# Weights cast to bf16 inside GpSimd DMAs, a shared head for two FFN blocks, and scan PSUM in two slots

## The chip, the cores and the metric

One core of one Trainium2 chip. The metric is the device time of one execution in microseconds (us), lower is better. Executions of one kernel mostly agree within 0.3%, though in this case several kernels spread more, so comparisons use the fast runs and carry a 95% interval. A run more than 1.5% above the fastest of its kernel is called slow and is left out of ratios.

## The reference, cut to what matters

A Mamba-2 scan (4 batches, 8 heads, 768 tokens, head size 32, state size 16), whose output, 3,072 tokens of 256 channels, goes through a feed-forward network (FFN) with a squared ReLU.

```python
for c in range(nc):                      # chunks of 32 tokens
    M = einsum(Cc, Bc) * L               # L: causal mask times decays
    y = M @ xc + (Cc @ state) * exp(cum)
    state = decay_full * state + sum(B x * decay_from_j)
x = y.transpose(0, 2, 1, 3).reshape(3072, 256)
h = np.maximum(x @ w_in, 0.0)            # w_in  256 x 2048, float32, 2.1 MB
out = (h * h) @ w_out                    # w_out 2048 x 256, float32, 2.1 MB
```

## The kernel before

It works in 12 blocks of 256 tokens. For each block GpSimd prepares `cz`, `Bb`, `xs` in bf16; TensorE transposes (`tr`), VectorE copies the result out of PSUM (`bct`); TensorE makes `U` (state input) and `mt` (the C·B products); VectorE makes the state `S` and the masks `mts`; TensorE adds up `Y`; ScalarE copies it out as `T`, the FFN's input. The FFN of a block is eight steps. A step is a group of four products with w_in (`mm1`), a ReLU on ScalarE, a square on VectorE, and, LAG steps later, a group of four with w_out (`mm2`). The scan of block k is strewn among the FFN steps of block k-1, starting LEAD steps ahead.

```python
LAG, LEAD = 4, 12
ps_h = pool(bufs=2)   # PSUM, FFN up-projection      (cut to what matters)
ps_o = pool(bufs=2)   # PSUM, FFN down-projection
ps_s = pool(bufs=1)   # PSUM, scan: ONE slot of four banks
...
def load_wi(f0, f1):  # float32 into a staging tile, SyncE's queue
    nc.sync.dma_start(out=w_in_f[:, :, f0*128:f1*128], in_=...)
def cast_wi(f0, f1):
    nc.scalar.copy(out=w_in_b[...], in_=w_in_f[...])
def cast_wo(f0, f1):
    nc.gpsimd.tensor_copy(out=w_out_b[...], in_=w_out_f[...])
...
# all on SyncE's queue, which moves them in this order
load_wi(0, 2); load_wi(2, 4); ph_load(1); load_wi(4, 8); load_wo(0, 4)
load_wi(8, 12); ph_load(2); load_wi(12, 16)
load_wo(4, 8); load_wo(8, 12); load_wo(12, 16); ph_load(3)
...
for s in range(len(steps) + LAG):
    if s < len(steps):
        mm1(*steps[s])
    for fn, args in todo.pop(s, []):     # scan pieces, casts
        fn(*args)
    if 1 <= s <= len(steps):
        square(*steps[s - 1])
    if LAG <= s < len(steps):
        mm2(*steps[s - LAG])
```

## Time and profile before

| | before |
|---|---|
| median (3 runs, when predicted) | 131.44 us (131.12 to 132.25) |
| span of the profiled execution | 129.1 us |
| TensorE busy | 116.4 us, 90% of the span |
| first FFN product | 14.06 us |
| a steady block of 256 tokens | 8.90 us, TensorE busy in all of it |

Below, the head is the first 34 us or so, in which weights arrive and the scan starts up, and the steady part is what follows. One row that the prediction did not look at, of this kernel's table of 40 slices (each digit is the clock granted to TensorE in tenths of full speed), is needed later:

```profile
PEclk9999999999999999999999999999999999999999
```

### The profile page before, as it was taken

To read this page: it belongs to the slowest core of one execution; us is meant where nothing else is said; L and a number is where in the kernel's file an instruction comes from. 1 tells how busy PE (TensorE), PEld (TensorE's weight loads), DVE (VectorE), ACT (ScalarE), POOL (GpSimd) and SP (SyncE) were. 2 spreads that over 40 slices of the span, in tenths; PEclk is the share of its full clock that TensorE was granted. 3 is DMA by queue.
4 is the path that set the end of the run, shared out by engine and by line. 5 is a ranking of instruction groups with operands and counts; after the bars stand their busy time and mean duration, and the time that the engine had idled before them with its cause. 6 is when DMAs were issued, how large, how long until landed. Compare 5 with 4: busy or idle time off the path is not lost.

```text
span 129.1 us, 4225 instructions
## 1 busy us (share of the span) xinstructions
PE 116.4 (90%) x1776; PEld 90.8 (70%) x1776; DVE 90.9 (70%) x203; ACT 75.6 (59%) x132; POOL 33.2 (26%) x56
## 2 busy tenths in 40 slices
PE   6697675896799999999999999999999999999980
PEld 4444443574687788778787877887787788788850
DVE  1338698499595796895995986977967848654421
ACT  2422784646357658467476576574775765776830
POOL 4045333659540051060150070440600000000000
PEclk9999999999999999999999999999999999999999
DMA  4999989988900550831903805607401020020201
GB/s 91 239 220 286 300 176 303 322 151 180 188 7 5 136 110 5 179 70 40 202 9 95 152 2 121 128 5 160 87 30 59 5 84 0 5 81 0 86 25 57
DMA packets 43172, 14.20 MB, mean 110 GB/s; under 512 B 37840, under 2 KB 40976, under 8 KB 43152
## 3 DMA queue, kind: packets, MB, share of 16 engines
q1 hardware_dynamic: 41712, 13.47, 44.9%
q10 hardware_dynamic: 1440, 0.45, 1.7%
q8 instruction: 14, 0.23, 0.8%
q14 instruction: 6, 0.05, 0.1%
HBM read 10.77 MB, written 3.15 MB: 108 GB/s over the span
## 4 chain that ended last, share of the span: by engine, by line
PE 69%; DVE 9%; SPq 9%; DMA 7%; ACT 2%; issue 1%; DVEq 0%; ACTq 0%
PE ops L334 29%; PE hps L314 27%; SPq L119 8%; DMA w_in_f<-in_moe_w_in_dram 4%; DVE mts L210 4%; DVE h L324 3%; PE Y L286 3%; PE mt L199 3%; DMA B_nat<-in_B_dram 3%; PE Y L274 3%; PE tr L187 2%; PE U L234 1%; PE ops L347 1%; PE tr L185 1%; ACT hb L318 1%
## 5 line engine op out<-in xcount | busy, mean ns | idle before, releaser
L318 ACT ACTIVATE hb<-hps 128x512 bf16<-128x512 f32 x96 | 57.5, 599 | 34.6 <-PE hps L314 33.1
L314 PE MATMUL hps<-T,w_in_b 128*128 128x256 bf16 x384 | 57.7, 273 | 2.0 <-ACT w_in_b L135 1.3
L334 PE MATMUL ops<-w_out_b,h 128*128 128x256 bf16 x368 | 55.5, 273 | 0.1
L324 DVE TENSOR_TENSOR h<-hb 128x512 bf16<-128x512 bf16 x96 | 46.1, 501 | 6.7 <-ACT hb L318 6.6
L314 PEld LDWEIGHTS <-w_in_b 128*128 128x128 bf16 x384 | 37.1, 98 | 7.2 <-ACT w_in_b L135 2.0
L334 PEld LDWEIGHTS <-h 128*128 128x128 bf16 x368 | 33.2, 98 | 7.0 <-issue 2.2
L210 DVE TENSOR_TENSOR mts<-mt,cb 128x512 bf16<-128x512 f32 x46 | 30.5, 685 | 4.5 <-PE mt L199 2.5
L146 POOL TENSOR_TENSOR cz<-C_nat,P_sb 128x256 bf16<-128x256 f32 x11 | 7.5, 679 | 42.0 <-DMA C_nat<-in_C_dram 36.1
L189 DVE COPY bct<-tr 128x768 bf16<-128x768 bf16 x12 | 6.7, 558 | 13.7 <-PE tr L187 13.7
L166 POOL TENSOR_TENSOR xs<-x_nat,Pinv 128x512 bf16<-128x512 f32 x12 | 13.5, 1125 | 9.4 <-DVE Pinv L409 5.1
L390 PE MATMUL dps<-dum 128*128 128x256 bf16 x36 | 7.6, 379 | 1.1 <-DVE dum L382 1.1
L303 ACT CAST T<-Y 128x512 bf16<-128x512 f32 x11 | 6.4, 586 | 2.1 <-PE Y L286 1.0
L160 POOL CAST Bb<-B_nat 128x128 bf16<-128x128 f32 x22 | 6.9, 343 | 2.2 <-DMA B_nat<-in_B_dram 1.2
L274 PE MATMUL Y<-bct,S 32*32 32x128 bf16 x160 | 4.4, 217 | 2.6 <-DVE mts L210 2.5
L390 PEld LDWEIGHTS <-dum 128*128 128x128 bf16 x36 | 4.5, 136 | 2.8 <-DVE dum L382 1.0
L359 ACT COPY osb<-ops 128x512 f32<-128x512 f32 x11 | 6.4, 580 | 0.0
L274 PEld LDWEIGHTS <-S 32*32 32x32 bf16 x160 | 2.5, 90 | 5.2 <-issue 4.8
L286 PE MATMUL Y<-mts,xs 64*32 64x128 bf16 x384 | 5.2, 219 | 0.8 <-DVE mts L216 0.8
L185 PE MATMUL tr<-cb,Bb 128*128 128x128 bf16 x24 | 4.9, 227 | 1.1 <-ACT T L303 1.1
L138 POOL CAST w_out_b<-w_out_f 128x1024 bf16<-128x1024 f32 x4 | 4.2, 1040 | 6.5 <-DMA w_out_f<-in_moe_w_out_dram 6.5
L187 PE MATMUL tr<-cb,cz 128*128 128x128 bf16 x48 | 5.6, 226 | 0.0
L199 PE MATMUL mt<-bct 32*64 32x256 bf16 x192 | 5.5, 291 | 0.0
(39 smaller groups left out, 46.5 us busy)
## 6 DMA issues: line engine op xcount, KB each, us to landing
x_nat<-in_x_dram SPq DMA_DIRECT2D x12, 256.0 KB, 4.4
out_dram<-osb SPq DMA_DIRECT2D x11, 256.0 KB, 2.2
w_out_f<-in_moe_w_out_dram SPq DMA_DIRECT2D x4, 512.0 KB, 6.5
C_nat<-in_C_dram SPq DMA_DIRECT2D x12, 128.0 KB, 4.0
w_in_f<-in_moe_w_in_dram SPq DMA_DIRECT2D x3, 512.0 KB, 5.6
B_nat<-in_B_dram SPq DMA_DIRECT2D x11, 128.0 KB, 3.9
w_in_f<-in_moe_w_in_dram SPq DMA_DIRECT2D x2, 256.0 KB, 4.9
B_nat<-in_B_dram ACTq DMA_DIRECT2D x1, 128.0 KB, 3.3
```

The lines of the kernel that those rows point to most:

```text
L119: (eng or nc.sync).dma_start(out=dst, in_=_dap(src, (b * NH * S + j * 256) * w, [[2 * w, 128], [S * w, NH], [1, 2 * w]]))
L166: eng.tensor_tensor(out=_fap(xs, 0, [[256, 2], [32, 8], [1, 32]]), in0=_fap(loaded[k]["x"], 0, [[32, 2], [64, 8], [1, 32]]), in1=_fap(Pinv ...
L187: nc.tensor.transpose(tr[:, r, 1 + g, :], v["cz"][:, r, 112 * g:112 * g + 128], eye_b)
L199: nc.tensor.matmul(mt[64 * u:64 * u + 64, q, r, :, :], bct[32 * q:32 * q + 32, r, 0, u * 64:u * 64 + 64], _fap(bct[32 * q:32 * q + 32], 12 ...
L210: nc.vector.tensor_tensor(out=v["mts"][:, q], in0=v["mt"][:, q], in1=_fap(cb, 128, [[128, 2], [0, 2], [1, 128]]), op=ALU.mult)
L274: nc.tensor.matmul(Y[u][32 * q:32 * q + 32, g, :], S_b[32 * q:32 * q + 32, g * 32:(g + 1) * 32], _fap(v["bct"][32 * q:32 * q + 32], 128 + ...
L286: nc.tensor.matmul(Y[u][32 * q:32 * q + 32, g, :], v["xs"][64 * u:64 * u + 64, r, h * 32:h * 32 + 32], v["mts"][64 * u:64 * u + 64, q, r, ...
L314: nc.tensor.matmul(hps[:, i, :], w_in_b[:, g, f * 128:(f + 1) * 128], T[blk][:, g].rearrange("p r u t -> p (r u t)"), start=(g == 0), stop ...
L318: nc.scalar.activation(out=hb, in_=hps, func=AF.Relu)
L324: nc.vector.tensor_tensor(out=h2, in0=hb, in1=hb, op=ALU.mult)
L334: nc.tensor.matmul(ops[blk][:, r, :], h2[:, i, r * 128:(r + 1) * 128], w_out_b[:, f, :], start=(f == 0 and r == 0), stop=(f == 15), skip_g ...
L390: nc.tensor.matmul(dps, dum[:, 0:128], dum, start=True, stop=True, skip_group_check=True)
```

## The change

Its intent: ScalarE and GpSimd no longer cast the weights, since the DMA does it; two FFN blocks share the first weights, so that they are needed half as fast; and the scan's PSUM is two slots of two banks, so that one phase of the scan need not wait until the other's tile is empty. With it come a reordered prologue, squares one step later, and a scan that starts two steps later. Below, "lag 1" and "lag 2" say how many steps after its ReLU a square is issued (the constant LAG, for the down-projection, stays 4), and "lead 12" and "lead 10" give LEAD.

```diff
-    LEAD = 12
+    LEAD = 10
-    ps_s = pool(bufs=1)                      # four banks
+    ps_s = pool(bufs=2)                      # two banks each; mt is two tiles
     def load_wi(f0, f1):
-        nc.sync.dma_start(out=w_in_f[...], ...)
+        nc.gpsimd.dma_start(out=w_in_b[...], ...)      # load_wo likewise
-    def cast_wi(...), cast_wo(...), and all their calls
...
         ph_load(1); ph_load(2); ph_load(3)   # SyncE: weights no longer in between
         for i in range(3):
             nc.gpsimd.memset(cz[i], 0.0)
+        load_wi(0, 4); load_wi(4, 8); load_wo(0, 4)
...
         prep_c(1, nc.gpsimd); prep_b(1, nc.gpsimd); prep_x(1, nc.gpsimd)
+        load_wi(8, 16); load_wo(4, 8); load_wo(8, 16)
...
-        warm(14) ... warm(3) ... warm(4) ... warm(3) ... warm(12)
+        warm(15) ... warm(4) ... warm(5, 128) ... warm(14, 128)
...
+        head = [(0, 0), (0, 1), (0, 2), (0, 3), (0, 4), (1, 0), (1, 1), (1, 2), (1, 3),
+                (0, 5), (1, 4), (0, 6), (1, 5), (0, 7), (1, 6), (1, 7)]
+        steps = head + [(b, f) for b in range(2, NPAIR) for f in range(8)]
...
-            if 1 <= s <= len(steps):
-                square(*steps[s - 1])
+            if 2 <= s < len(steps) + 2:
+                square(*steps[s - 2])
```

Cut: the second state of block 0 and one reciprocal moved to later, the first mask taken from its own PSUM tile, positions of block 2's scan pieces.

## The prediction

> **What bounds the kernel now.** I read the page's per-slice table first, then windows, the chain of waits, and a timeline of the first 34 us. The slices (columns are fortieths of the span, 3.23 us each, in tenths busy):
>
> ```profile
> PE   6697675896799999999999999999999999999980
> DVE  1338698499595796895995986977967848654421
> DMA  4999989988900550831903805607401020020201
> ```
>
> The reader is to see two kernels. From slice 12 on TensorE is full and nothing else matters; before it TensorE has holes and the DMA engines are the row that is full. The windows put microseconds on it (start:end, length, then busy time and count for PE, PEld, DVE, ACT, POOL, then clock, DMA share, GB/s):
>
> ```profile
> 0.00:14.00 14.00, 10.43 (x118) 6.45 (x118) 6.17 (x18) 4.42 (x10) 4.87 (x12) 1.00 1.01 223
> 14.00:24.00 10.00, 6.68 (x119) 4.49 (x120) 7.05 (x14) 7.32 (x12) 4.11 (x6) 1.00 0.98 261
> 24.00:33.00 9.00, 7.10 (x125) 5.39 (x122) 8.17 (x14) 4.78 (x9) 6.93 (x11) 1.00 0.92 191
> ...
> 50.50:59.40 8.90, 8.90 (x152) 7.11 (x151) 7.38 (x17) 5.74 (x11) 2.19 (x4) 1.00 0.42 90
> ...
> 122.80:129.10 6.30, 2.52 (x21) 1.63 (x18) 1.08 (x3) 0.97 (x2) 0.00 (x0) 1.00 0.12 42
> ```
>
> A steady block of 256 tokens takes 8.90 us with TensorE busy for all of it. So what the change does after about 34 us is worth nearly nothing; the game is in the first 34 us, where TensorE is idle 3.3 + 1.9 us in the two middle windows, plus whatever the 14 us of prologue can be shortened by (its 10.43 us busy are mostly dummy warm-up products). The timeline names the holes:
>
> ```profile
> 8.96 1.07 ACT L417 CAST mts<-mt 128x512 bf16<-128x512 f32 x2 [2.66 <-PE mt L199]
> 10.07 1.29 DVE L210 TENSOR_TENSOR mts<-mt,cb 128x512 bf16<-128x512 f32 x2 [2.05 <-ACT mts L417]
> ...
> 12.97 0.41 PE L286 MATMUL Y<-mts,xs 64*32 64x128 bf16 x30 [0.80 <-DVE mts L216]
> ...
> 14.06 0.60 PE L314 MATMUL hps<-T,w_in_b 128*128 128x256 bf16 x4 [0.69 <-DVE T L299]
> ...
> 19.49 1.22 DVE L324 TENSOR_TENSOR h<-hb 128x512 bf16<-128x512 bf16 x1
> ...
> 21.36 0.29 PE L274 MATMUL Y<-bct,S 32*32 32x128 bf16 x8 [1.36 <-DVE mts L210]
> ```
>
> ```profile
> 31.72 0.29 PE L274 MATMUL Y<-bct,S 32*32 32x128 bf16 x8 [1.13 <-DVE mts L210]
> ...
> 33.10 0.22 PE L185 MATMUL tr<-cb,Bb 128*128 128x128 bf16 x1 [0.74 <-ACT T L303]
> ```
>
> To be seen: in the prologue VectorE's first mask waits 2.05 us, until ScalarE has copied the other half of the same PSUM tile; the FFN's first product starts at 14.06; block 1's Y products wait for VectorE's masks until 21.36 and block 2's until 31.72; the next transposes wait for the one PSUM tile to be emptied. In the list of waits the casts of w_in on ScalarE also hold TensorE: 2.0 us in 3 waits on the weight-load side, 1.3 us in 3 on the product side, overlapping. None of them is in the steady part.
>
> **What the Trainium skill says.** (1) "TensorE: Matmul & The Clock Gate", Part 1: a warm product costs N / 2.4 GHz plus about 2.5 ns, so 256 columns 109 ns and a group of four 0.437 us. The trace agrees: the chain alternates FFN groups every 0.44 us. (2) "DMA: Bandwidth & Descriptors", section SWDGE vs HWDGE vs iDMA: a cast in the DMA must come from GpSimd, whose cores write the descriptors; the Specifications give a first byte after about 1 us against 0.6. The kernel before has no such DMA, so no trace shows it yet. (3) The same page, "Issuing engines are not separate DMA queues": all queues share the same 16 DMA engines. The DMA row agrees: two queues are in use at the start, and the sum is full. (4) "SBUF — State Buffer", Who interferes with whom: a VectorE instruction with two SBUF inputs contends with a GpSimd one that reads SBUF. The trace agrees: the square at 19.49 took 1.22 us instead of about 0.42 while GpSimd's xs (19.37 to 20.43) ran.
>
> **The change part by part.**
>
> *Casts removed.* ScalarE loses two casts of 0.62 us and three of 1.04 us, 4.4 us; GpSimd four of 1.04 us, 4.2 us. ScalarE's lie in the head and hold TensorE in part. HBM still has to give 4 MB of f32, so the reading side of the DMA does not shrink: over 0 to 27 us it moved about 6.5 MB at 240 GB/s (from the windows). The order changes: scan inputs first on the SP queue, 1.5 MB of weights beside them from GpSimd at about 2.1 us (end of its memsets), the other 2.5 MB only after block 1's preparation on GpSimd.
>
> *Prologue.* The f32 constants go first on ScalarE's queue instead of second: the transposes of the decay waited for them until 5.2, now about 0.5 to 0.7 us less. Masks: the products' output is now two tiles, so the first mask need not wait for ScalarE's copies. Chain after the products, worked from the rows: mask 0.65, state 0.28, mask 0.65, two bf16 masks 0.74, about 2.5 us with handovers, so Y can start near 11.5 where everything before stays in place, against 12.97: 1.4 us. With the constants 2.0; I take 1.8 because new waits will show. First FFN product: 14.06 becomes about 12.3.
>
> *From the first FFN product to block 1's Y.* Before: 7.3 us (14.06 to 21.36), set by VectorE: T copy, bct 0.56, three small state operations 0.8, four masks 2.75, three squares and the contention. The new lag of two steps takes one square (0.42) out of this chain and some of the contention (0.8); the postponed second state of block 0 puts 0.55 back. About 6.4 us, so 0.9 gained. But TensorE now has only the five first groups of block 0 queued before that Y, where it did six and one down-projection group: 2 x 0.437 = 0.9 us of work is pushed behind it. These cancel.
>
> *After block 1's Y.* Before, at 21.36, 185 of 192 groups were left, 80.8 us; plus Y of block 1, 0.75; plus ten scans at 8.90 - 16 x 0.437 = 1.91, 19.1 us. Sum 100.7, so a full TensorE would end at 122.0; the last products ended at about 125.9. Loss 3.9 us, of which about 0.7 is the last relu and square, which stay. The new kernel keeps: T of block 1 feeding the next product directly, 0.9 less one group = 0.5; block 2's Y behind masks and the postponed 0.94 us reciprocal, about 1.0; late weights 0.4 (see rivals). 1.9 instead of 3.1, gain 1.2.
>
> *Shared slices.* Block 0 and 1 use the slices in turn, so weights are needed half as fast. By itself it saves no TensorE time; it is what lets block 1's FFN fill while the last 2.5 MB arrive.
>
> *Two PSUM slots, lead 10, in the steady part.* TensorE is already 8.90 busy in 8.90; gain at most 0.1 per block, which I put at 0.2 in all and lose in rounding.
>
> Sum: 1.8 + 0.9 - 0.9 + 1.2 = 3.0, and 0.2 more: 131.4 - 3.2 = 128.2.
>
> **The rivals.**
>
> *Weights late.* The second w_in half is issued only at about 10.5 us, behind GpSimd's xs of block 1, with 1 MB and the down weights after it. At the 240 GB/s that the windows show, shared with the remaining scan inputs, I estimate it at 17 to 18, and TensorE needs it at step 4, before Y of block 1 in its order. The last w_out needs 2.5 MB plus what is left of the scan inputs, 3.5 MB / 240 GB/s = 14.5 us, about 24 to 25, and is wanted at step 8, about 23. For it: the DMA row is full to slice 10 now. Against: fewer small packets are left by then, and the window from 12 to 15 us reached 355 GB/s. If casting DMAs are slower than plain ones, 2 to 4 us are lost here: 130 to 132.
>
> *GpSimd becomes the wait.* Three descriptor jobs between 2.1 us and the first xs, which before began at 7.20. At 1 us each they end near 5; at 2 us each they delay U, the state and Y: 129 to 130.
>
> *VectorE's chain stays as long.* If Y of block 1 still comes 7.3 us after the first product, the two pushed-back groups cost 0.9: 129.3. If instead the head is cleaner than I think and nearly all 3.1 us of later loss goes, 126.
>
> *Nothing moves, because the DMA bytes bound the head.* 4 MB f32 still come in; if the end of weights sets the start of full flow, the gain is only the saved casts, about 1 us: 130.4.
>
> **Range and chances.** Point 128.2; the terms' errors (prologue 1, weights 1.5, chain 1) give 125.9 to 130.6. The line for faster by over 2% is 128.8, close to the point; the prior that such a reordering was tuned against the clock pushes a bit my way. Faster 0.61, within 2% 0.33, slower 0.06.
>
> **What would show it.** First FFN product at about 12.3 (prologue right) or still near 14 (wrong); first mask no longer released by ScalarE's copy; Y of block 1 near 18.7; no wait of TensorE on w_in or w_out DMAs over 0.5 us; block 2's Y with a wait of about 1 us; steady blocks still 8.8 to 8.9. A long stretch of GpSimd before the first xs, or TensorE waits released by weight DMAs, would make the prediction wrong on the high side; a steady block well under 8.8 on the low side.

## The result, and the profile after

The changed kernel is correct and slower.

| | before | after |
|---|---|---|
| median (4 runs each) | 131.84 us | 137.00 us |
| lowest to highest | 131.12 to 132.34 | 135.91 to 138.74 |
| ratio of fast runs | | 1.037 (1.026 to 1.047) |
| profiled span | 129.1 us | 134.7 us (fast state) |

Ratios here and below are the mean time of one kernel's fast runs over that of the other's fast runs in the same rounds, so they are not quite the ratio of the medians quoted.

First the changed kernel's table of slices (3.37 us each):

```profile
PE   6868914999999998998999979999999999999980
PEclk9995595599999999999999999999999999999996
DMA  4999999950003980811902802704602020020201
```

TensorE is nearly idle in the sixth slice, its clock is at half in four of the first eight, and single slices of the steady part fall to 7 or 8. The windows of the changed kernel, in the columns of the prediction (start:end, length, busy of PE, PEld, DVE, ACT, POOL, then clock, DMA share, GB/s):

```profile
14.00:24.00 10.00, 5.23 (x90) 2.44 (x88) 6.40 (x13) 2.43 (x6) 6.43 (x11) 0.67 1.17 168
24.00:33.00 9.00, 9.00 (x97) 6.88 (x96) 4.66 (x11) 4.75 (x8) 3.31 (x5) 0.84 0.75 107
...
50.50:59.40 8.90, 8.32 (x144) 6.23 (x142) 6.76 (x17) 5.16 (x10) 3.57 (x7) 1.00 0.41 92
59.40:68.30 8.90, 8.42 (x144) 6.24 (x142) 6.49 (x17) 5.72 (x10) 1.54 (x5) 1.00 0.43 91
...
77.20:86.20 9.00, 8.10 (x137) 6.46 (x122) 6.76 (x15) 5.47 (x10) 1.32 (x3) 1.00 0.30 61
```

Two places lose. In 14 to 24 us TensorE does 5.23 us of work where it did 6.68, at a mean clock of 0.67: 17 products of the FFN against 36. From 24 to 33 us it is busy all the time and makes part of that good, 59 products of the FFN against 48, at a mean clock of 0.84. (The counts of the windows, 97 against 125, mix these with the scan's smaller products, so they can't be compared.) From the FFN's start to 33 us it has done 81 where the kernel before had done 84. Then the steady windows shown lack 0.58, 0.48 and 0.90 us, where before none lacked more than 0.07; from 86 us on they are full again. TensorE's timeline of the changed kernel names the first loss:

```profile
12.38 1.01 PE L304 MATMUL hps<-T,w_in_b 128*128 128x256 bf16 x4 [0.65 <-DVE z L241]
...
16.61 0.61 PE L304 MATMUL hps<-T,w_in_b 128*128 128x256 bf16 x4
21.99 1.04 PE L304 MATMUL hps<-T,w_in_b 128*128 128x256 bf16 x4 [4.77 <-DMA w_in_b<-in_moe_w_in_dram]
22.95 0.40 PE L264 MATMUL Y<-bct,S 32*32 32x128 bf16 x8
...
24.67 1.06 PE L304 MATMUL hps<-T,w_in_b 128*128 128x256 bf16 x4
25.52 1.06 PE L324 MATMUL ops<-w_out_b,h 128*128 128x256 bf16 x4
```

The FFN starts at 12.38 instead of 14.06, as hoped, and after four steps TensorE stands 4.77 us for the second half of w_in. Afterwards a group of four takes about 0.85 us (24.67 to 25.52) where the full clock gives 0.44. The chain of waits of the changed kernel says why w_in came so late (start, length, what):

```profile
5.10 8.36 DMA x_nat<-in_x_dram
13.53 0.89 POOL xs L157
14.54 7.41 DMA w_in_b<-in_moe_w_in_dram
21.99 1.04 PE hps L304 x4
```

Read it upwards. The load took 7.41 us, but it was also issued only at 14.54, because GpSimd issues in program order and the three loads stand behind `xs` of block 1. That waited for `x`, which had been 8.36 us on its way: it shares the 16 DMA engines with the first weights, which now come through a second queue beside it. Before, SyncE's queue carried these inputs and the weights in order, and the same `x`, issued at 5.85, landed after 5.2 us. GpSimd's timeline of the changed kernel shows the same queue of work from the engine's side:

```profile
12.34 0.53 POOL L151 CAST Bb<-B_nat 128x128 bf16<-128x128 f32 x2 [2.52 <-DMA B_nat<-in_B_dram]
13.53 1.06 POOL L157 TENSOR_TENSOR xs<-x_nat,Pinv 128x512 bf16<-128x512 f32 x1 [0.66 <-DMA x_nat<-in_x_dram]
14.54 0.77 POOL L122 DMA_DIRECT2D w_in_b<-in_moe_w_in_dram  x1
```

What the wait for issue meant for the DMA engines shows in a window of 3 us in which, after the change, the queue of weights was empty. Before, then after:

```profile
12.00:15.00 3.00, 1.51 (x44) 1.17 (x44) 2.20 (x5) 1.19 (x3) 0.37 (x2) 1.00 1.07 355
```

```profile
12.00:15.00 3.00, 2.62 (x30) 1.80 (x30) 1.20 (x4) 0.80 (x3) 2.00 (x4) 0.50 0.82 141
```

355 GB/s fell to 141 in the very stretch in which the weights should have come: only the scan inputs, in small packets, were in flight.

The second loss is named by the rows of the groups for the down-projection (busy, mean ns of one, idle just before, what ended it), products (PE) and weight loads (PEld), before and after:

```profile
L334 PE MATMUL ops<-w_out_b,h 128*128 128x256 bf16 x368 | 55.5, 273 | 0.1
...
L334 PEld LDWEIGHTS <-h 128*128 128x128 bf16 x368 | 33.2, 98 | 7.0 <-issue 2.2
```

```profile
L324 PE MATMUL ops<-w_out_b,h 128*128 128x256 bf16 x368 | 56.5, 277 | 2.1 <-DVE h L314 2.1
...
L324 PEld LDWEIGHTS <-h 128*128 128x128 bf16 x368 | 32.5, 99 | 11.7 <-DVE h L314 4.8
```

The squares `h` are what TensorE loads as weights for these products. Loads now wait 4.8 us in all for squares, where before squares ended no notable wait, and 2.1 us of it come through to the products as plain idleness; the rest stretches the distance between groups. VectorE's timeline in one steady block of the changed kernel shows how:

```profile
47.76 0.94 DVE L242 TENSOR_SCALAR S<-z,Ptot 128x64 bf16<-128x64 f32 x1
...
49.90 1.28 DVE L201 TENSOR_TENSOR mts<-mt,cb 128x512 bf16<-128x512 f32 x2
51.09 0.41 DVE L314 TENSOR_TENSOR h<-hb 128x512 bf16<-128x512 bf16 x1
```

The square of 51.09 stands behind two masks and is done at 51.50; TensorE, which wanted it, starts at 51.56 after a wait of 0.48 us. The state's multiplication took 0.94 us instead of the 0.25 of its sibling, beside GpSimd's `xs` (47.60 to 48.66): with the scan started later, GpSimd's preparation now falls upon this chain. The other traces bear this out: with lead 12 (the kernel before, experiments 3 and 11) every such multiplication after 44 us takes 0.25 to 0.26 us, while with lead 10 several take longer, up to 0.94 us here and 1.15 us in experiment 2.

How the two losses compare is read from ScalarE's timeline, at the copies that begin when a block's last product is done. The second block's copy, when both kernels have done the FFN of two blocks, and the copy of the last block but one, before and then after:

```profile
41.68 0.58 ACT L359 COPY osb<-ops 128x512 f32<-128x512 f32 x1
...
119.84 0.58 ACT L359 COPY osb<-ops 128x512 f32<-128x512 f32 x1
```

```profile
42.63 0.59 ACT L349 COPY osb<-ops 128x512 f32<-128x512 f32 x1
...
125.30 0.58 ACT L349 COPY osb<-ops 128x512 f32<-128x512 f32 x1
```

The head is only 0.95 us late at its end. The nine blocks after it take 82.67 us instead of 78.16, 4.5 us more. By the same copies, the first four of the nine take 9.5 to 9.95 us each, where before they took 8.9, and so lose 3.4 us; the next four take 8.95 as before, and the ninth 7.83 instead of 6.98. One reservation: with the later start of the scan a bit of scan work that was done by then before is now done after.

### The profile page after: what moved, and what is told of

Read it like the earlier page. It is cut to its first block, busy times and chain, and to the rows that moved or that the text cites. A ratio compares the mean times of both kernels' runs of the same rounds, so it can differ in the third digit from the quotient of the medians.

```text
span 134.7 us, 4221 instructions
## 1 busy us (share of the span) xinstructions
PE 120.2 (89%) x1778; PEld 91.2 (68%) x1778; DVE 86.9 (65%) x203; ACT 72.8 (54%) x127; POOL 32.0 (24%) x58
## 3 DMA queue, kind: packets, MB, share of 16 engines
q1 hardware_dynamic: 38240, 9.28, 33.7%
## 4 chain that ended last, share of the span: by engine, by line
PE 62%; DVE 19%; DMA 12%; SPq 3%; issue 1%; ACT 1%; POOL 1%; DVEq 0%
PE ops L324 26%; PE hps L304 24%; DVE mts L201 7%; DMA x_nat<-in_x_dram 6%; DVE h L314 6%; DMA w_in_b<-in_moe_w_in_dram 5%; PE Y L276 3%; DVE S L242 3%; SPq L116 3%; PE Y L264 2%; PE tr L178 2%; DVE z L241 2%; PE U L219 1%; PE mt L190 1%; PE ops L337 1%
## 5 line engine op out<-in xcount | busy, mean ns | idle before, releaser
L304 PE MATMUL hps<-T,w_in_b 128*128 128x256 bf16 x384 | 60.0, 281 | 5.4 <-DMA w_in_b<-in_moe_w_in_dram 4.8
L324 PE MATMUL ops<-w_out_b,h 128*128 128x256 bf16 x368 | 56.5, 277 | 2.1 <-DVE h L314 2.1
L314 DVE TENSOR_TENSOR h<-hb 128x512 bf16<-128x512 bf16 x96 | 41.5, 457 | 11.1 <-ACT hb L308 11.1
L304 PEld LDWEIGHTS <-w_in_b 128*128 128x128 bf16 x384 | 38.2, 100 | 11.5 <-DMA w_in_b<-in_moe_w_in_dram 5.1
L324 PEld LDWEIGHTS <-h 128*128 128x128 bf16 x368 | 32.5, 99 | 11.7 <-DVE h L314 4.8
L157 POOL TENSOR_TENSOR xs<-x_nat,Pinv 128x512 bf16<-128x512 f32 x12 | 13.1, 1090 | 12.6 <-DMA x_nat<-in_x_dram 11.9
L151 POOL CAST Bb<-B_nat 128x128 bf16<-128x128 f32 x22 | 5.8, 292 | 7.6 <-DMA B_nat<-in_B_dram 6.6
L374 PE MATMUL dps<-dum 128*128 128x256 bf16 (+1 forms) x38 | 6.2, 335 | 1.1 <-DVE dum L363 1.1
L242 DVE TENSOR_SCALAR S<-z,Ptot 128x64 bf16<-128x64 f32 x16 | 5.5, 346 | 0.6
L241 DVE TENSOR_TENSOR z<-U,S 128x64 f32<-128x64 f32 x16 | 3.6, 225 | 1.9 <-PE U L219 1.6
L190 PEld LDWEIGHTS <-bct 32*64 32x64 bf16 x192 | 2.3, 105 | 3.7 <-DVE z L241 1.5
```

The source lines that it names most:

```text
L157: eng.tensor_tensor(out=_fap(xs, 0, [[256, 2], [32, 8], [1, 32]]), in0=_fap(loaded[k]["x"], 0, [[32, 2], [64, 8], [1, 32]]), in1=_fap(Pinv ...
L190: nc.tensor.matmul(mt[q // 2][64 * u:64 * u + 64, q % 2, r, :, :], bct[32 * q:32 * q + 32, r, 0, u * 64:u * 64 + 64], _fap(bct[32 * q:32 * ...
L242: nc.vector.tensor_scalar(out=S_n, in0=z, scalar1=ptot, scalar2=None, op0=ALU.mult)
L304: nc.tensor.matmul(hps[:, i, :], w_in_b[:, g, f * 128:(f + 1) * 128], T[blk][:, g].rearrange("p r u t -> p (r u t)"), start=(g == 0), stop ...
L314: nc.vector.tensor_tensor(out=h2, in0=hb, in1=hb, op=ALU.mult)
L324: nc.tensor.matmul(ops[blk][:, r, :], h2[:, i, r * 128:(r + 1) * 128], w_out_b[:, f, :], start=(f == 0 and r == 0), stop=(f == 15), skip_g ...
```

## The experiments

**The theory.** The loss is two separate things: weights that arrive late in the head, since their issue waits behind block 1's preparation, and a steady part in which squares one step later and a scan two steps later leave too little time between a square and the product that wants it. **The rivals.** The casting DMAs are slower whenever they are issued; the two PSUM slots cost; the thinner warm-up lets the clock fall, and that alone makes the head slow; the scan inputs of later blocks steal the bandwidth. "Changed kernel" below means the one after the change. The experiments were built in sets (1 to 4, 5 to 8, 9 to 12, 13 to 15, 16 and 17), and those of one set share their runs of the kernel before.

**1. The second batch issued earlier.**

```diff
         prep_x(0, nc.gpsimd)
+        load_wi(8, 16); load_wo(4, 8); load_wo(8, 16)
...
         prep_x(1, nc.gpsimd)
-        load_wi(8, 16); load_wo(4, 8); load_wo(8, 16)
```

> The second batch of weights (2.5 MB) is issued by GpSimd right after block 0's xs, at about 9.1 us, instead of behind block 1's preparation at 14.54. Theory (late issue holds TensorE at step 4): the w_in load lands 7.4 us after issue, so near 17 us; the 4.77 us wait of TensorE on w_in goes to under 1 us, the clock does not fall at 20 us, and the time is 4 to 6 us under the changed kernel, 131 to 133. Rival (the DMA engines are simply full, so an earlier issue only makes block 1's inputs later): w_in still lands after 20 us and the time changes by less than 1.5 us.

133.7 us (133.18 to 140.62), ratio 1.020 (1.013 to 1.027): a gain of about 3 us, a little short of the 131 to 133 expected. The profile fell on a slow run, so it serves only for what it waited for: no wait for w_in is left, but TensorE waits 3.3 us each for `Bb` and for `xs` of block 1, whose inputs the earlier weights had pushed back. So lateness of issue costs, and moving all of it forward moves part of the wait to the scan's inputs.

**2 and 3. Squares one step sooner; the scan two steps sooner.**

```diff
-            if 2 <= s < len(steps) + 2:
-                square(*steps[s - 2])
+            if 1 <= s <= len(steps):
+                square(*steps[s - 1])
```

> The square again one step after its relu, all else as changed. Theory (the two-step lag puts squares behind the masks on VectorE and TensorE waits for them in the steady blocks): the blocks between 41 and 86 us lose the waits of the down-projection on the square, 2.1 us in the changed kernel, time minus 1.5 to 2.5. Rival (the waits come from GpSimd's preparation falling together with the state and mask chain, because the lead is shorter): the waits stay within 0.5 us of 2.1 and the time within 0.7.

134.95 us, ratio 1.030 (1.022 to 1.039).

```diff
-    LEAD = 10
+    LEAD = 12         # and block 3's scan starts at step 14
```

> The scan of blocks 4 to 11 two steps earlier again (lead 12), all else as changed. Rival of the run before: the waits of the down-projection on the square go from 2.1 us to under 0.5, time minus 1.5 to 2.5. If the two-step lag is the cause, they stay at 1.5 or more.

135.08 us, ratio 1.032 (1.020 to 1.043). In the profiles the nine blocks from the second block's copy to that of the last but one take 80.20 us with the sooner squares and 79.91 with the sooner scan (changed kernel 82.67, before 78.16): each alone brings back more than half. The products' waits for squares, 2.1 us in the changed kernel, are gone in both (0.0 and 0.1 us), so the two are not rivals: it takes both to make these waits, and the two-step lag alone (experiment 3) leaves only 2.6 us of waits of the weight loads, of 4.8. The wait for w_in is still there in both, 5.9 and 5.5 us, a little longer than it was. The medians fell by 2 us as expected, the ratios by only half a per cent, with intervals that overlap the changed kernel's, so the times alone would not have settled it.

**4. The warm-up as full as before.** The dummy products back to 256 columns, and five more of them in all (the recorded text says seven; the two programs have 38 and 43).

```diff
-        warm(5, 128) ... warm(14, 128)
+        warm(5) ... warm(12)      # and warm(3) before U, warm(4) before tr
```

> Dummy products of full width again and seven more of them in the prologue. Theory (the prologue's thinner warm-up lets the clock fall to half at about 9 us, and that costs something): the granted clock stays 1.0 from 0 to 15 us; block 1's transposes come 0.5 to 1 us earlier; but as w_in's second half is awaited until 22 us anyway, the time changes by less than 1 us. Rival (the half clock in the prologue is a main loss): time minus 2 us or more.

137.59 us, ratio 1.048 (1.038 to 1.057): no gain. The clock now stays at full until about 18 us, and then falls anyway, during a wait for w_in of 6.6 us. The head got to the missing weights sooner and stood there longer.

**5. The casting DMAs alone**, in the kernel before: its prologue, PSUM, order of blocks, lag and lead, with the weights loaded as the changed kernel loads them and no casts on the engines.

```diff
-    load_wi(...); load_wo(...)     # SyncE's queue, with casts on ScalarE and GpSimd
+    load_wi(0, 4); load_wi(4, 8); load_wo(0, 4)        # after the memsets on GpSimd
+    load_wi(8, 16); load_wo(4, 8); load_wo(8, 16)      # after prep_x(1) on GpSimd
```

> The kernel before with only the weights changed: cast by GpSimd DMAs in the changed kernel's pieces and at its places, the engine casts gone. Theory (the loss comes from taking the weights out of the one ordered queue): this alone is slower than before by 2 to 5 us, TensorE waits over 2 us on a w_in load. Rival (the shared head, lag and lead do the harm, the cast DMAs are neutral or a gain): within 1 us of before or faster.

132.96 us, ratio 1.015 (1.009 to 1.021). A wait for w_in of 3.8 us appears in the kernel before too. So the loads by themselves cost 1.5%, even with ScalarE and GpSimd freed of 8.6 us of casts.

**6. The reverse: the changed kernel with float32 loads in the old order and casts on the engines.**

```diff
-        nc.gpsimd.dma_start(out=w_in_b[...], ...)
+        nc.sync.dma_start(out=w_in_f[...], ...)        # old order; cast_wi, cast_wo back
```

> The changed kernel with the weights taken back: f32 loads in the order of the kernel before on the SP queue, and the casts on ScalarE and GpSimd. Theory: no TensorE wait on w_in over 1 us, the clock stays full after 16 us, and the time is at or under the kernel before, 129.5 to 132, with the steady waits of about 2 us still in it. Rival: it stays over 134.5.

137.32 us, ratio 1.049 (1.042 to 1.056). A clear miss: without casting DMAs the changed kernel is as slow as with them. Its profile shows that the old order of loads does not suit the shared head, which wants w_out while w_in 12 to 16 is still useless to it: TensorE waits 2.2 us for a cast of w_out whose load came at 24.60, and the steady waits for squares are still there (2.5 us). Two causes in one run; experiments 10 and 13 part them.

**7. The second batch in smaller pieces, in the order of need, at the same place.**

```diff
-        load_wi(8, 16); load_wo(4, 8); load_wo(8, 16)
+        load_wi(8, 10); load_wi(10, 12); load_wo(4, 8); load_wi(12, 16); load_wo(8, 16)
```

> The changed kernel with its second batch of weights in smaller pieces in the order of need (w_in 8-10, 10-12, w_out 4-8, w_in 12-16, w_out 8-16), issued at the same place. Theory (step 4 needs slices 8 and 9 alone, but waits for a load of 1 MB): the first piece, a quarter of it, lands some 3 to 5 us earlier, the first w_in wait falls from 4.8 to about 1 us, and the time falls by 2 to 4 us. Rival (latency of a full set of DMA engines, not the size of the piece): the wait stays over 3.5 us.

136.89 us (135.2 to 138.13), unclear: two of the four runs are fast (135.2 and 135.66; the changed kernel's fast ones lay at 135.91 to 137.52), so at most a gain of about 1 us, and no ratio is on record. The wait for w_in fell from 4.8 to 1.7 us as foreseen, and part of the gain was lost elsewhere: TensorE waits 1.8 us for masks and 1.2 us for w_out. One line of VectorE in this run explains the masks:

```profile
18.61 2.61 DVE L314 TENSOR_TENSOR h<-hb 128x512 bf16<-128x512 bf16 x1
```

A square takes 2.61 us instead of 0.42. GpSimd, busy since 14.94 with five descriptor jobs, ends the last at 18.78 and goes straight on to block 2's `cz`, `Bb` and `xs` until 20.93. So 0.17 us of the square lie beside the descriptors and nearly all the rest beside the preparation that, as I read it, they had pushed there.

**8. The inputs of blocks 2 to 4 held back**, to leave the engines to the weights.

```diff
-        ph_load(1); ph_load(2); ph_load(3)
+        ph_load(1)            # 2, 3, 4 from ScalarE's queue at steps 0, 4, 10
```

> The changed kernel with the inputs of blocks 2, 3 and 4 issued from ScalarE's queue behind its work at steps 0, 4 and 10, so that they no longer run beside the weights and block 1's inputs from 7.8 us on. Theory (the scan inputs on the SP queue take DMA time in turn with the weights): w_in's second half lands in about 5 us instead of 7.4, the w_in wait is 2 us or less, time minus 2 to 4 us. Rival: the weights' own descriptors or the casting set the pace, the load still takes 7 us and the wait stays.

140.64 us, ratio 1.071 (1.062 to 1.080): the worst of all. The load of w_in 8 to 16 still took 8.6 us, with hardly anything but block 2's inputs beside it. But these, now issued at 13.8 to 14.9 us, still moved about as much beside the weights (0.51 MB in 15 to 23 us) as all scan inputs did in the changed kernel (0.48 MB in 15 to 22). So the run did not take that traffic away, and whether it slows the load stays untested; only the inputs of blocks 3 and 4 are cleared. The run adds a cost of its own: ScalarE held up by issuing DMAs (a wait of 1.6 us for `T`), and its profile is of the slow state.

**9. The third part alone:** new prologue and two PSUM slots, everything else (weights, order, lag, lead) as before.

> The third part alone: the changed prologue and the two PSUM slots, with the weights, block order, lag and lead of the kernel before. Theory (the losses lie in the weights' DMAs, the shared head and the lag and lead; this part is a gain, as the first FFN product at 12.4 instead of 14.1 shows): 129 to 130.5, 1 to 2 us under the kernel before, steady blocks at 8.9. Rival (the slots or the thinner warm-up harm): over 131.5.

```diff
-    head = [...]; steps = head + [...]                 # the plain order of blocks again
-    nc.gpsimd.dma_start(out=w_in_b[...], ...)          # SyncE loads and casts again
+    LEAD = 12; square(*steps[s - 1])                   # lag and lead again
```

131.47 us (20 runs, 18 fast), ratio 0.9998 (0.997 to 1.003). Neutral together; no run parts the prologue from the slots, so a gain of one and a loss of the other is not ruled out. In the profile, which is of a slow run, the FFN starts at 12.59, so the prologue does what it should, and then TensorE waits 4.4 us for casts of w_in, whose loads come no earlier than they did. Here a head that starts sooner than its weights gained nothing.

**10. A shared head with loads in its own order of need.** Float32 loads on SyncE's queue, casts on the engines, lag 1, lead 12 and the full warm-up.

```diff
         load_wi(4, 8); load_wo(0, 4)
-        load_wi(8, 12); ph_load(2); load_wi(12, 16)
-        load_wo(4, 8); load_wo(8, 12); load_wo(12, 16); ph_load(3)
+        load_wi(8, 12); load_wo(4, 8); load_wo(8, 12)
+        ph_load(2); load_wi(12, 16); load_wo(12, 16); ph_load(3)
```

> The shared head with f32 loads on the SP queue in the order in which the head needs them (w_out 4-12 ahead of block 2's inputs, w_in 12-16 behind), engine casts, lag 1, lead 12, full-width warm-up. Theory (the run of the shared head without cast DMAs was slow because its loads stood in the wrong order for it, its clock fell, and its steady part kept the waits): 129 to 131.5, at or under the kernel before. Rival (sharing slices itself costs, since block 1's scan and the interleaving put more waits into the head): 132.5 or more.

129.42 us (128.56 to 130.72; three fast runs), ratio 0.984 (0.975 to 0.994). Faster than both kernels. About 4 us of waits for casts of w_in are left.

**11. Lag 1 and lead 12 together** in the changed kernel, casting loads and all.

```diff
-    LEAD = 10
+    LEAD = 12
-                square(*steps[s - 2])
+                square(*steps[s - 1])
```

> The changed kernel with lag 1 and lead 12 together. Theory (lag and lead are two remedies of one wait, 2.1 us of down-projections waiting for squares): the gains do not add up, about 2 to 2.5 us under the changed kernel, 134.5 to 135, with no wait of a down-projection on a square after 36 us. Rival (two separate causes): 133 or less.

132.94 us, ratio 1.012 (1.005 to 1.020). Better than expected: from 1.037 to 1.012 is 2.4%, 3.2 us (give or take 1.7 us by the two intervals), more than the 2 us that I had expected from the idle time of 2.1 us in the row of products. The expectation that the two gains would not add fell: singly they gave 0.7% and 0.5%, and the rival, two separate causes and 133 us or less, came true in the times. The nine blocks take 78.55 us, 4.1 us less than in the changed kernel and 0.4 more than before. Its windows, where the changed kernel had 8.32 and 8.42, are full:

```profile
50.50:59.40 8.90, 8.90 (x152) 7.15 (x150) 7.30 (x19) 5.75 (x10) 2.34 (x5) 1.00 0.43 92
59.40:68.30 8.90, 8.90 (x152) 7.13 (x150) 7.47 (x18) 5.74 (x10) 2.15 (x4) 1.00 0.43 91
```

The wait for w_in is there as ever, 5.5 us, and the second block's copy comes at 43.33, 0.7 us later than in the changed kernel, which is about what the sooner scan moves into the head. 4.1 less 0.7 is the 3.4 us by which the two profiled spans differ (134.7 and 131.3).

**12. As 11, with w_in 8 to 12 issued before block 1's preparation and the full warm-up.**

```diff
         prep_x(0, nc.gpsimd)
+        load_wi(8, 12)
...
-        load_wi(8, 16); load_wo(4, 8); load_wo(8, 16)
+        load_wo(4, 8); load_wi(12, 16); load_wo(8, 16)
```

> Cast DMAs kept: w_in 8-12 is issued right after block 0's xs, the rest stays behind block 1's preparation in the order w_out 4-8, w_in 12-16, w_out 8-16; lag 1, lead 12, full-width warm-up. Theory (the software queue stood empty from 12 to 14.5 us, and step 4 needs 512 KB of it alone): the first w_in wait is under 1.5 us, the clock holds, 130 to 132.5. Rival (any weight issued earlier delays block 1's inputs as much as it gains): over 133.

130.61 us (20 runs), ratio 0.995 (0.992 to 0.998). No wait for w_in; now 2.1 us for w_out and 3.3 us for masks (in a profile of the slow state, 132.53 us).

**13 to 15. Which of the mended things did it?** 13 is number 10 with the old order of loads; 14 is number 10 with the changed kernel's thin warm-up; 15 is number 12 with the thin warm-up.

```diff
 # 13
-        load_wi(8, 12); load_wo(4, 8); load_wo(8, 12); ph_load(2); load_wi(12, 16)
+        load_wi(8, 12); ph_load(2); load_wi(12, 16); load_wo(4, 8); load_wo(8, 12)
 # 14 and 15
-        warm(5) ... warm(12)
+        warm(5, 128) ... warm(14, 128)
```

> The fastest version so far (f32 loads, casts on engines, shared head, short lag, early scan start, full-width warm-up: 129.4 us, ratio 0.984), but with the loads in the order of the kernel before instead of the order in which the shared head needs them. Theory, order of arrival decides the head: the product with w_out again waits for its first late cast, as in the version with old order and nothing else mended (137.3, 2.2 us there): 131.5 to 133.5, ratio 1.00 to 1.015. Rival, the gain came from lag, lead and warm-up, whatever the order: 129 to 130, ratio 0.98 to 0.99.

132.4 us, ratio 1.007 (1.005 to 1.010). The order, with the cast of w_out 8 to 12 that moves with it from step 4 to step 6, is worth 2.3% between 13 and 10, and the wait for a cast of w_out is back (2.9 us in two waits). Against number 6, which has the same loads in the same order, lag, lead (with block 3's earlier start) and warm-up gave 4%.

> The fastest version so far with the changed kernel's thinner warm-up (narrow dummy products, fewer of them) put back. Theory, the granted clock of the head costs 1 to 2 us by itself: 130.5 to 131.5, ratio 0.993 to 1.00, and the clock falls before 14 us in the profile. Rival, the clock falls on the wait for w_in at about 19 us whatever was before: 129 to 130, no difference.

128.77 us (127.70 to 130.09), ratio 0.972 (0.964 to 0.981). The theory falls: the thin warm-up is no worse than the full one. The profiles show why it need not be: in 10, at full clock, TensorE is ready for the fifth group of products at about 16.05 and waits 3.02 us for its weights; in 14, with groups of twice the length (1.01 to 1.06 us), it is ready at 17.4 and waits 1.61 us. They start at 19.06 and 18.98.

> The changed kernel with lag 1, lead 12 and one cast piece of w_in moved before block 1's preparation, but with its own thin warm-up. With the full warm-up this was 130.6 (0.995), without early piece and warm-up 132.9 (1.012). If the early piece gave the gain: 130.5 to 131.2, ratio 0.995 to 1.00. If the warm-up gave it: 132 to 133, ratio 1.005 to 1.012.

131.56 us (20 runs), ratio 0.994 (0.990 to 0.998), against 0.995 with the full warm-up. The warm-up gave nothing, so the gain from 1.012 is the early piece's. How large it is, is less sure: 11 of the 20 runs count as slow and are left out, and the median of all 20 (131.56) is that of all runs of the kernel before in the same rounds (131.67) to 0.1%.

**16. Number 14 with the other 23 dummy products taken away**, since three pairs had now shown no worth in the warm-up while groups at half clock were plain to see.

```diff
-        warm(4) ... warm(5, 128) ... warm(14, 128)
```

> The fastest version so far (128.8 us, ratio 0.972) with all dummy products taken away after the first 15 (23 fewer). Theory, TensorE's clock in the head is worth time: the clock is at half over most of 10 to 17 us, the first products of the FFN take twice as long, 129.8 to 131, ratio 0.98 to 0.99. Rival, the head is bound by what arrives and a half clock only fills waits: 128 to 129.3, ratio 0.967 to 0.978.

129.25 us, ratio 0.981 (0.973 to 0.988). The interval overlaps that of number 14 and lies between the two expectations, so if the dummy products are worth anything here it is under about 1%. TensorE's timeline of this run shows that it is at half clock and that the wait for w_in is gone:

```profile
15.07 1.04 PE L313 MATMUL hps<-T,w_in_b 128*128 128x256 bf16 x4
16.04 0.65 PE L199 MATMUL mt<-bct 32*64 32x256 bf16 x16
16.62 1.72 PE L313 MATMUL hps<-T,w_in_b 128*128 128x256 bf16 x8
18.43 0.29 PE L273 MATMUL Y<-bct,S 32*32 32x128 bf16 x8
```

In number 14, also at half clock, the same place has a wait of 1.61 us, and its `Y` comes a microsecond later:

```profile
18.98 0.61 PE L313 MATMUL hps<-T,w_in_b 128*128 128x256 bf16 x4 [1.61 <-ACT w_in_b L135]
19.52 0.29 PE L273 MATMUL Y<-bct,S 32*32 32x128 bf16 x8
```

The clock is not the reason: TensorE is ready for these weights at about 17.4 in both. ScalarE began to cast the piece at 16.64 in 16 and at 17.87 in 14, since its load landed 7.5 us after its issue instead of 8.7, and no run says why. Number 16 then loses the lead again to masks (2.1 us in three waits).

**17. Number 14 with w_in 8 to 12 loaded ahead of w_out 0 to 4**, to take away that last wait of 1.61 us.

```diff
-        load_wo(0, 4); load_wi(8, 12)
+        load_wi(8, 12); load_wo(0, 4)
```

> The fastest version so far with w_in 8 to 12 loaded ahead of w_out 0 to 4, since the one wait left in its head (1.6 us at 17.4 to 19.0) is for the cast of that piece. Theory, each wait for weights in the head adds to the end: wait gone, 127.3 to 128.2, ratio 0.962 to 0.968. Rival, the waits only move (to w_out 0 to 4 on GpSimd or to the masks): 128.5 to 129.5, ratio 0.972 to 0.98.

130.09 us, ratio 0.989 (0.984 to 0.993): slower than number 14. The wait fell to 0.56 us, but VectorE's masks took its place (2.7 us in three waits), as two squares and GpSimd's casts of w_out now fell together (1.21 us for a square instead of 0.42). The profile is of the slow state, so the sizes are only a hint; the verdict rests on the times. The rival was right in direction, but the loss is larger than it said (0.972 to 0.98).

**Put together.** Each row is a ratio to the kernel before:

| version | ratio |
|---|---|
| whole change | 1.037 |
| casting loads alone (5) | 1.015 |
| prologue and PSUM slots alone (9) | 1.000 |
| whole change, lag 1 and lead 12 (11) | 1.012 |
| ... and w_in 8 to 12 issued early (15) | 0.994 |
| ... or float32 loads in the order of need (14) | 0.972 |

The fastest version keeps the shared head, the prologue and the two slots, and takes back the casting loads, the lag and the lead. It is 2.8% faster than the kernel before (0.964 to 0.981, from three fast runs, the best of seventeen versions). No run takes the shared head away from it, so what the shared head gives and what the order of loads gives is not parted; with the old order it was 0.7% slower than the kernel before (13).

## Why the prediction was wrong

The prediction said 128.2 us, 61% for faster, and a range up to 130.6; measured were 137.0.

*Prologue: right.* First FFN product predicted "about 12.3", measured 12.38; the first mask no longer waits for ScalarE. Even the remark that new waits would show came true: the transposes wait 0.77 us for the bf16 constants. But experiment 9 shows that this start, with the two slots, was worth nothing without sooner weights.

*"Late weights 0.4 (see rivals)" in the sum: the first step that failed.* It was mis-sized by more than ten times. Measured: 4.77 us of wait, and more behind it. The working put the issue "at about 10.5 us" and the landing "at 17 to 18"; they were 14.54 and 21.94. The 4 us by which the issue was late are two errors. In the kernel before, `xs` of block 1 ran from 11.13 to 12.19, so 10.5 was too early even for the old time, by about 1.7 us. The other 2.3 us or so are `x`, which came at 13.46 instead of about 11.1, as the change put 1.5 MB of weights beside the scan's inputs. The skill page "DMA: Bandwidth & Descriptors", Queues, rings and completion order, says that each engine takes packets from its queues by turns; the prediction had cited that all queues share the engines, and did not draw the conclusion that `x` of block 1 would slow down (8.36 us against 5.2). The load itself took what the prediction allowed, about 7 us. "No wait of TensorE on w_in or w_out DMAs over 0.5 us" was named as the sign, and it failed. The rival "Weights late", at 130 to 132, named the place, an issue behind `xs` of block 1 and TensorE at step 4 without w_in, but the condition it set for a loss, casting DMAs slower than plain ones, is not what these lines show. Its size fits the casting loads alone (132.96 us, 1.5% or 2.0 us, experiment 5).

*The granted clock: a step that was not there at all.* After the 4.77 us, TensorE works at half clock. Four groups, from 21.99 to 22.95 and from 23.84 to 26.38, took 3.50 us; at 0.437 us each they would take 1.75. This fits "TensorE: Matmul & The Clock Gate", Part 1, by which an idle window of about 3.4 us halves the clock. The half clock from about 10 us on, before the wait, it does not explain: between 4.4 and 9.7 us TensorE's longest gap is 0.77 us, and why the clock fell there stays open. I first blamed the thin warm-up, and the pairs 10 and 14, and 12 and 15, show no time lost by it: in 14 the slower TensorE only waits less for the same weights. Since no run sets the clock by itself, the 1.75 us behind the wait are what the lines show and not a tested effect.

*Two PSUM slots, lead 10, in the steady part: the second step that failed.* It was predicted as "at most 0.1 per block, which I put at 0.2 in all", a gain, and the new square lag was counted only in block 1's chain, as a gain too. The runs show that lag and lead together cost 2.4%, 3.2 us (changed kernel against experiment 11) in the times, and 4.1 us of the nine steady blocks in the profiles; and that the slots with the prologue are neutral (experiment 9). The reasoning was that a full TensorE can't get fuller. It forgot that it can get emptier, since what it loads as weights comes from VectorE. VectorE is not busier than before (6.76 us of 8.90 against 7.38); what is used up is the time between a square and the product that wants it, two steps instead of three. "Steady blocks still 8.8 to 8.9" was the sign: the first four of the nine took 9.5 to 9.95 us. The slots are cleared only together with the prologue, though the steady windows of experiment 11, which has them, are full.

*Casts removed: right in count, and no gain to be seen.* 8.6 us of casts leave ScalarE and GpSimd, and the kernel with only that and the casting loads is 1.5% slower (experiment 5). No run takes the casts away and leaves the loads, so what they are worth alone is not shown. "4 MB f32 still come in" was right too. The rival with these words, at 130.4, saw the gain vanish but not turn into a loss.

*From the first product to block 1's `Y`* (6.4 us predicted, so 18.7) can't be tested, as the wait for w_in lies in it: `Y` began at 22.95.

*The sum.* By ratios, 3.7% of about 131.7 us is 4.8 us lost. 3.2 us of it is lag and lead, the larger part by the middle values (the intervals leave 1.7 us either way), although the one wait of 4.77 us is the more striking line. The other 1.6 us, the ratio of experiment 11, is the head: 5.5 us of wait for w_in there, paid for in part by the earlier start and by waits of the kernel before which are gone (2.5 us for block 1's and block 2's masks, 1.3 us for casts of w_in).

What stays open: what the half clock behind the wait would be worth by itself; whether the scan inputs beside the weights slow them; and what the casting route costs if it were issued in the ideal order. Between 15 and 14 lie 2.2%, but 15's order is still bound by where GpSimd is free to issue.

## What to carry to other kernels

A DMA issued from a compute engine starts when that engine gets to it: before moving loads there, write down the work ahead of them and what that work waits for, and check that order of arrival equals order of need. A reordering that frees the bottleneck in the head may take away, in the steady part, the time between a neighbour's result and its use, so ask of a full engine not only whether it can gain but what keeps it full. And part a bundled change before judging it: here the casting loads cost, the later squares and scan cost more, the prologue with the slots was neutral, and the best version keeps the shared head, the prologue and the slots and drops the rest.

## What the Trainium skill lacked or had wrong

- "DMA: Bandwidth & Descriptors", Rules for kernel authors, says to issue a cast from GpSimd and gives it no price. Here the weights took 11.0% of 134.7 us on 16 engines, 14.8 us, as casting loads; as float32 loads the main queue's time was larger by 44.9% of 129.1 less 33.7% of 134.7, 12.6 us. So the casting loads took some 18% more engine time in this kernel. That is an estimate: it is a sum of packet times, which two queues that share the engines may lengthen too, and the cast was not tested apart from that (the queue rows are below, before then after).

```profile
q1 hardware_dynamic: 41712, 13.47, 44.9%
```

```profile
q1 hardware_dynamic: 38240, 9.28, 33.7%
q0 software_dynamic: 2912, 2.10, 11.0%
```

- The same page, Anatomy of one DMA, fits 2.0 us plus bytes over 436 GB/s to one such DMA; for the 1 MB of w_in 8 to 16 that is 4.4 us, an estimate from the page's fit. Here, with a cast and beside another queue's traffic, it took 7.41 us, and 8.6 us in experiment 8. The page's own table of bandwidth has 6.15 us for 1 MB, nearer to these than its fit. It calls the time for descriptors small; here GpSimd spent 0.72 to 0.90 us on each load.
- "SBUF — State Buffer", Who interferes with whom, is right about the contention, and by the same page's Summary the second to issue blocks until the first finishes. In experiment 7 a square of 0.42 us took 2.61 us, about the length of three preparation steps of GpSimd in a row: I found no page which says that the waiting instruction can lose several times. That is how the line reads; no run tested it by itself.
- "TensorE: Matmul & The Clock Gate", Part 1, calls the warm-up penalty under 1% of a typical kernel. Experiments 10, 12, 14, 15 and 16 agree (no loss that the runs can tell). Nothing is lacking on the wait in mid-kernel: the page's HAM oscillation section tells of the half clock that follows a wait for a DMA, and here four groups took twice their length after 4.77 us, 1.75 us or 1.3% of the span.
